# One kernel, a linear-attention block beside a gated feed-forward: K weights on ScalarE's DMA queue, normalisation shared out to VectorE and ScalarE, spare matmuls in another bank, a new order at the start, denominators spread differently

## The chip, the cores, the metric

One core of one Trainium2 chip runs the program. The metric is the device time of one execution in microseconds (us). Each comparison runs both kernels in alternation on the same chip. "Clock" is the mean share of TensorE's full clock that was granted in a run.

## The reference, cut to what matters

```python
xn = _layernorm(x)                        # x: 1 x 2048 x 576, bf16
def _A_ref(x, wqkv, wo):                  # linear attention, 32 heads of 18
    q, k, v = ...(x @ wqkv)...
    phi = lambda t: where(t > 0, t + 1, exp(t)) + 1e-6
    kv = einsum("bhsd,bhse->bhde", phi(k), v);  z = sum_s phi(k)
    o = (phi(q) @ kv) / (phi(q) . z + 1e-6)
    return o @ wo
def _B_ref(x, w_gate, w_up, w_down):      # F = 4608
    return (gelu(x @ w_gate) * (x @ w_up)) @ w_down
return x + _A_ref(xn, wqkv, wo) + _B_ref(xn, w_gate, w_up, w_down)
```

## The kernel before

The 2048 tokens are 16 tiles of 128. The kernel has an attention stage (to about 70 us), then four passes of 512 tokens, each with 18 blocks of gate and up matmuls and then the down projection. I call the steps of tile n: **Tn** its transposes on TensorE, **Kn** and **Qn** its ten K and ten Q matmuls with five in each half, **Gn** the seven matmuls that add its phi(k) and xn products up in PSUM. K0 needs x of tile 0: statistics on VectorE, reciprocal root on ScalarE, normalisation, T0, a copy out of PSUM in two parts (one on ScalarE, one on VectorE).

```python
nc.scalar.preload_act_table_set("natural_log_exp_and_others")
load_x(0, 1)            # SyncE's queue, in this order
load_x(1, 1)
load_w(1)               # K weights: rows 0-511, then rows 512-575
load_x(2, 2)
load_w(0)               # Q weights
load_x(4, 4)
...
def spin(count):        # spare matmuls, to keep TensorE's clock up
    nc.tensor.matmul(ps_all[:, 3, 0:P], lhsT=ident[:], rhs=ident[:], ...)
spin(NWARM)             # 38
...
def ln_norm(n, c0=0, c1=D):
    (nc.vector if n < TD else nc.gpsimd).tensor_scalar(...)   # TD = 3
...
TP_BANK = (3, 1, 0)     # PSUM banks of T0, T1, T2; G writes banks 0 to 3
```

The order of the attention stage on each engine is not written down; a list scheduler computes it in Python when the kernel is built. Each step has an engine, a duration, a rank and predecessors, and the loads are constants: the times from which x and the weights are believed to be there.

```python
X_AT = [2.95, 3.40, 6.20, 6.20] + [9.60] * 4
W_AT = {1: 5.60, 0: 7.90}
...
step(("stats", n, h), "DVE", 0.41, n - 2.2, after_x, ..., ready=x_at)
step(("aggr", n), "DVE", 0.21, n - 2.1, [("stats", n, 0), ("stats", n, 1)], ...)
...                     # cut: rstd, norm, tp, xnT, mm, exp, phi
step(("G", n), "PE", 0.75, n + 1.15, [("phi", n, 1, 0), ("phi", n, 1, 1)], ...)
```

Each engine then works through its instructions strictly in that order.

The denominators of the attention are computed on VectorE between the gated products of the feed-forward:

```python
nc.vector.tensor_tensor(out=hT[:, GUB * k + i, :], ...)    # gated product
if den_jobs and blk > 0:
    job, n = den_jobs.pop(0); job(n)
```

Of the kernel before, what the change touches and what calls it, by code (L numbers as in the profile page):

```python
# [8 lines left out]
ACT = mybir.ActivationFunctionType  # L9
ALU = mybir.AluOpType  # L10
BF16 = mybir.dt.bfloat16
F32 = mybir.dt.float32
# [3 lines left out]
P = 128  # L16
HP = 64
S = 2048
D = 576
# [3 lines left out]
NS = S // P  # L23
NF = F // P
# [11 lines left out]
GUB = 2  # L36
# [3 lines left out]
TD = 3  # L40
# [17 lines left out]
def kernel(  # L58
# [11 lines left out]
    nc = tc.nc  # L70
# [9 lines left out]
    persist = ctx.enter_context(tc.tile_pool(name="persist", bufs=1))  # L80
# [4 lines left out]
    ps_all = psum.tile([P, 8, 512], F32, name="ps_all")  # L85
# [4 lines left out]
    x_sb = persist.tile([P, NS, D], BF16, name="x_sb")  # L90

    def load_x(n0, cnt):
        nc.sync.dma_start(x_sb[:, n0:n0 + cnt, :], x_view[:, n0:n0 + cnt, :])  # L93
# [8 lines left out]
    wqkv_sb = apool.tile([P, KT, 3 * D], BF16, name="wqkv_sb")  # L102


    def load_w(which):
        c = slice(which * D, (which + 1) * D)
        nc.sync.dma_start(wqkv_sb[:, 0:4, c], A_wqkv[0:512, c].rearrange("(kt p) c -> p kt c", p=P))
        nc.sync.dma_start(wqkv_sb[0:HP, 4, c], A_wqkv[512:576, c])

    nc.scalar.preload_act_table_set("natural_log_exp_and_others")  # L110
    load_x(0, 1)
    load_x(1, 1)
    load_w(1)
    load_x(2, 2)
    load_w(0)
    load_x(4, 4)

    nc.vector.memset(wqkv_sb[HP:P, 4, :], 0.0)

    ident = const.tile([P, P], BF16, name="ident")  # L120
# [8 lines left out]
    def spin(count):  # L129

        for _ in range(count):
            nc.tensor.matmul(ps_all[:, 3, 0:P], lhsT=ident[:], rhs=ident[:], start=True, stop=True)

    spin(NWARM)

    xnT = persist.tile([P, KT, S], BF16, name="xnT")
# [15 lines left out]
    def load_gu(i, part):  # L152
# [17 lines left out]
    xn = apool.tile([P, NS, XW], BF16, name="xn")  # L170
# [9 lines left out]
        out=bm3, in_=bm3, compare_op=ALU.is_ge, fill=0.0,  # L180
# [3 lines left out]
        out=bm3, in_=bm3, compare_op=ALU.is_ge, fill=0.0,  # L184
# [8 lines left out]

    mv = persist.tile([P, NS, nc.vector.BN_AGGR_DIM], F32, name="mv")
    rstd = persist.tile([P, NS], F32, name="rstd")

    ln_raw = {}

    def ln_half(n, h):
        if h == 0:  # L200
            ln_raw[n] = asmall.tile([P, 2, nc.vector.BN_STATS_DIM], F32, name="stats")
        nc.vector.bn_stats(out=ln_raw[n][:, h, :], in_=x_sb[:, n, h * HALF:(h + 1) * HALF])  # L202

    def ln_aggr(n):
        nc.vector.bn_aggr(out=mv[:, n, :], in_=ln_raw[n][:])

    def ln_rstd(n):
        r = rstd[:, n:n + 1]
        nc.scalar.activation(out=r, in_=mv[:, n, 1:2], func=ACT.Ln, bias=eps_ln[:], scale=1.0)
        nc.scalar.activation(out=r, in_=r, func=ACT.Exp, scale=-0.5)  # L210

    def ln_norm(n, c0=0, c1=D):
        (nc.vector if n < TD else nc.gpsimd).tensor_scalar(  # L213
            out=xn[:, n, c0:c1], in0=x_sb[:, n, c0:c1], scalar1=mv[:, n, 0:1], scalar2=rstd[:, n:n + 1],
            op0=ALU.subtract, op1=ALU.mult,
        )
# [3 lines left out]
    def tp_bank(b):  # L220
        return ps_all[:, b, :].bitcast(BF16).rearrange("p (k t) -> p k t", t=P)
# [3 lines left out]
    def transposes(n, k0=0, k1=KT, b=None):  # L225
        b = TP_BANK[n] if b is None else b
        for kt in range(k0, k1):
            nc.tensor.transpose(tp_bank(b)[:, kt, :], xn[:, n, kt * P:(kt + 1) * P], ident[:])

    def tp_copy(n, k0=0, k1=KT, b=None, copy=acopy):  # L230
        b = TP_BANK[n] if b is None else b
        copy(out=xnT[:, k0:k1, n * P:(n + 1) * P], in_=tp_bank(b)[:, k0:k1, :])  # L232

    def dma_transposes(n):
        nc.sync.dma_start_transpose(xnT[:, :, n * P:(n + 1) * P], xn[:, n, 0:640])
# [162 lines left out]
    def step(name, *args, **kw):  # L398
        steps[name] = _Step(*args, **kw)

    X_AT = [2.95, 3.40, 6.20, 6.20] + [9.60] * 4
    W_AT = {1: 5.60, 0: 7.90}

    for n0 in (8, 12):
        step(("x", n0), "SP", 0.50, n0 - 5.5, [], lambda n0=n0: load_x(n0, 4), ready=8.5, tail=3.0)
    for n in range(NS):
        after_x = [("x", n // 4 * 4)] if n >= 8 else []
        x_at = X_AT[n] if n < 8 else 0.0
        for h in range(2):
            step(("stats", n, h), "DVE", 0.41, n - 2.2, after_x, lambda n=n, h=h: ln_half(n, h), ready=x_at)  # L410
        step(("aggr", n), "DVE", 0.21, n - 2.1, [("stats", n, 0), ("stats", n, 1)], lambda n=n: ln_aggr(n))
        step(("rstd", n), "ACT", 0.49, n - 2.1, [("aggr", n)], lambda n=n: ln_rstd(n))
        if n == 0:
            for i, (k0, k1, b, eng) in enumerate([(0, 3, 3, "ACT"), (3, KT, 2, "DVE")]):
                step(("norm", n, i), "DVE", 0.25, n - 2.1 + i / 10, [("rstd", n)],
                     lambda k0=k0, k1=k1: ln_norm(0, k0 * P, min(k1 * P, D)))
                step(("tp", n, i), "PE", 0.20, n - 1.5, [("norm", n, i)], lambda k0=k0, k1=k1, b=b: transposes(0, k0, k1, b))
                step(("xnT", n, i), eng, 0.45, n - 2.1, [("tp", n, i)],
                     lambda k0=k0, k1=k1, b=b, eng=eng: tp_copy(0, k0, k1, b, acopy if eng == "ACT" else vcopy))
            ready = [("xnT", n, 0), ("xnT", n, 1)]  # L420
        elif n < TD:
            step(("norm", n), "DVE", 0.42, n - 2.1, [("rstd", n)], lambda n=n: ln_norm(n))
            step(("tp", n), "PE", 0.30, n - 1.5, [("norm", n)], lambda n=n: transposes(n))
            step(("xnT", n), "ACT", 0.69, n - 1.5, [("tp", n)], lambda n=n: tp_copy(n))
            ready = [("xnT", n)]
        else:
            step(("norm", n), "POOL", 0.80, n - 2.1, [("rstd", n)], lambda n=n: ln_norm(n))
            step(("xnT", n), "SP", 2.30, n - 1.9, [("norm", n)], lambda n=n: dma_transposes(n), tail=0.4)
            ready = [("xnT", n)]
        for which, rank in ((1, n), (0, n + 0.6)):  # L430
            for h in range(2):
                r = rank + h / 100
                free = [("phi", n - 1, which, h)] if n else []
                step(("mm", n, which, h), "PE", 0.615, r, ready + free, lambda n=n, w=which, h=h: kq_mm(n, w, h),
                     ready=W_AT[which], tail=0.15)
                step(("exp", n, which, h), "ACT", 0.45, r + 0.10, [("mm", n, which, h)],
                     lambda n=n, w=which, h=h: kq_exp(n, w, h))
                step(("phi", n, which, h), "DVE", 0.43, r + 0.15, [("exp", n, which, h)],
                     lambda n=n, w=which, h=h: kq_phi(n, w, h))
        step(("G", n), "PE", 0.75, n + 1.15, [("phi", n, 1, 0), ("phi", n, 1, 1)], lambda n=n: g_accumulate(n, G_A))  # L440
    for i, (at, count) in enumerate([(5.75, 3), (6.15, 4)]):
        step(("spin", i), "PE", 0.1 * count, -1.0, [], lambda count=count: spin(count), ready=at)

    def in_order(steps):
# [89 lines left out]
    den_jobs = [(job, n) for n in range(NS) for job in (den_mul, den_inv, den_scale, den_transpose)]  # L534

    def gu_pair(sc, k):
        cs = slice(sc * SC, (sc + 1) * SC)
        blk = sc * (NF // GUB) + k
        wg, wu, wr = gu_blocks.pop(blk)
        units = []  # L540
        for i in range(GUB):
            b = [banks.next(), banks.next()]
            fcol = slice(i * P, (i + 1) * P)

            def lhs(a, rows, kt, fcol=fcol):
                if kt == 4:
                    return wr[rows, fcol]
                return (wg, wu)[a][rows, kt, fcol]

            u = _Unit([ps_all[:, b[0], :], ps_all[:, b[1], :]], lhs, lambda a, rows, kt: xnT[rows, kt, cs],  # L550
                      nc.sync if blk == 0 else nc.gpsimd)
            if blk > 0:
                load_gu(blk + NWBUF - 1, i)
            u.p1()
            units.append((b, u))
        if sc == 0 and k == 1:
            load_wo()
        elif sc == 0 and k >= 2:
            load_wd_slice()
        for i, (b, u) in enumerate(units):  # L560
            u.p2()
            gl = fwork.tile([P, SC], F32, name="gl")
            nc.scalar.activation(out=gl[:], in_=ps_all[:, b[0], :], func=ACT.Gelu_apprx_tanh)  # L563
            nc.vector.tensor_tensor(out=hT[:, GUB * k + i, :], in0=ps_all[:, b[1], :], in1=gl[:], op=ALU.mult)  # L564
            if den_jobs and blk > 0:
                job, n = den_jobs.pop(0)
                job(n)

# [76 lines left out]
```

## Time and profile before

| | before |
|---|---|
| median of 3 runs | 520.57 us (520.33 to 520.65) |
| span of the profiled execution | 517.8 us |
| TensorE busy | 510.4 us |
| T0, K0, Q0, G0 begin at | 5.5, 7.1, 9.4, 12.6 us |
| G0 to first gate/up matmul | 58.1 us |
| first gate/up matmul to first small product (m stage) | 70.3 us |
| first small product to first matmul of pass 2 | 42.6 us |
| pass 2 to the last matmul | 330.6 us |

The last rows cut TensorE's timeline at four marks. As TensorE sets the end nearly everywhere, a part of the change shows up as a difference of one of these distances. A line of a timeline reads: start us, duration us, engine, source line, operation, output<-input, shape, count, and in brackets the idle time before and what ended it. The lines of TensorE and of the waits are in the prediction. What the argument will need besides is VectorE's timeline of the kernel before:

```profile
3.00 1.19 DVE L202 BATCH_NORM_STATS2 stats<-x_sb 128x6 f32<-128x288 bf16 x3 [1.04 <-DMA x_sb<-in_A_x_dram]
4.11 0.19 DVE L205 BATCH_NORM_AGGREGATE mv<-stats 128x2 f32<-128x12 f32 x1
...
4.90 1.16 DVE L213 TENSOR_SCALAR xn<-x_sb,mv,rstd 128x384 bf16<-128x384 bf16 x3
```

The aggregate's start, 4.11, is what matters; further statistics between it and the normalisation are left out. Three statistics run ahead of tile 0's aggregate: two of tile 0 and the first of tile 1. Tile 1's x has landed by 3.75 (issued at 1.25, 2.5 us to landing), so this costs 0.37 us (one statistics instruction, from its start to the next one's) and no more.

### The profile page before, as it was taken

Reading aid. Unit: us, or ns where it says so; the run is one execution under the profiler, and the core shown is the slowest. Engines: PE = TensorE matmul, PEld = TensorE weight load, DVE = VectorE, ACT = ScalarE, POOL = GpSimd, SP = SyncE. Lnnn points to the kernel's source line nnn. Section 1 sums busy time; section 2 is a strip of 40 time slices with the busy share of each in tenths; the row PEclk is TensorE's granted clock in tenths of the full one; section 3 lists DMA queues with packets and bytes.
Section 4 is the critical chain, followed back from the end, with each engine's and each line's share of the span. In section 5 each row is a group of like instructions: output and inputs, shape, how many; then the busy total and the mean of one; then the engine's idle time right before and its main releaser. Section 6 shows DMA issues by size and latency. Waiting matters only on the chain.

```text
span 517.8 us, 10582 instructions
## 1 busy us (share of the span) xinstructions
PE 510.4 (99%) x4497; PEld 314.2 (61%) x4497; DVE 202.0 (39%) x407; ACT 133.5 (26%) x260; POOL 36.0 (7%) x32
## 2 busy tenths in 40 slices
PE   7999999999999999999999999999999999999997
PEld 6788864447577744444577644444777544445775
DVE  6895446666610146766301043343101233333100
ACT  5676523223320013323200032332000133232000
POOL 3995000000000000000000000000000000000000
PEclk9999999999999999999999999999999999999999
DMA  8237619999910046658500155555000455540000
GB/s 285 53 70 153 150 28 226 282 263 273 250 38 13 13 115 169 191 149 178 140 11 13 50 159 161 155 143 160 26 22 13 122 156 148 156 121 2 13 11 24
DMA packets 117785, 60.86 MB, mean 118 GB/s; under 512 B 24810, under 2 KB 117162, under 8 KB 117738
## 3 DMA queue, kind: packets, MB, share of 16 engines
q1 hardware_dynamic: 117738, 60.19, 45.0%
q8 instruction: 35, 0.57, 0.5%
q14 instruction: 12, 0.10, 0.1%
HBM read 52.79 MB, written 2.36 MB: 107 GB/s over the span
## 4 chain that ended last, share of the span: by engine, by line
PE 94%; DMA 3%; SPq 1%; ACT 1%; DVE 0%; POOL 0%; issue 0%
PE ps_all L298 53%; PE ps_all L592 27%; PE ps_all L243 6%; PE ps_all L597 4%; PE ps_all L274 4%; DMA wqkv_sb<-in_A_wqkv_dram 1%; DMA wr<-in_B_w_up_dram 1%; DMA xnT<-xn 1%; POOL xn L213 0%; SPq L93 0%; PE ps_all L345 0%; DVE hT L564 0%; PE ps_all L574 0%; ACT phi_e L250 0%; DVE den_t L358 0%
## 5 line engine op out<-in xcount | busy, mean ns | idle before, releaser
L298 PE MATMUL ps_all<-xnT,wg 64*128 64x512 bf16 x1152 | 272.4, 376 | 0.0
L298 PE MATMUL ps_all<-xnT,wu 64*128 64x512 bf16 x1152 | 270.8, 376 | 0.0
L563 ACT ACTIVATE gl<-ps_all 128x512 f32<-128x512 f32 x144 | 86.0, 597 | 314.1 <-PE ps_all L298 311.7
L564 DVE TENSOR_TENSOR hT<-ps_all,gl 128x512 bf16<-128x512 f32 x144 | 99.4, 690 | 145.7 <-ACT gl L563 145.4
L298 PEld LDWEIGHTS <-wu 64*128 64x128 bf16 x1152 | 108.1, 94 | 66.0
L298 PEld LDWEIGHTS <-wg 64*128 64x128 bf16 x1152 | 108.2, 94 | 65.6
L592 PE MATMUL ps_all<-wd_sb,hT 128*128 128x288 bf16 x1152 | 147.0, 286 | 0.0
L592 PEld LDWEIGHTS <-hT 128*128 128x128 bf16 x1152 | 112.3, 98 | 30.4 <-issue 2.0
L600 DVE TENSOR_TENSOR res<-ps_all,x_sb 128x288 bf16<-128x288 f32 x32 | 14.6, 458 | 143.6 <-PE ps_all L597 143.6
L298 PE MATMUL ps_all<-xnT,wr 64*128 64x512 bf16 x288 | 56.2, 376 | 0.1
L243 PE MATMUL ps_all<-wqkv_sb,xnT 128*128 128x288 bf16 x320 | 42.5, 286 | 1.3 <-DMA wqkv_sb<-in_A_wqkv_dram 0.9
L243 PEld LDWEIGHTS <-xnT 128*128 128x128 bf16 x320 | 30.4, 98 | 9.0 <-issue 1.1
L250 ACT ACTIVATE phi_e<-ps_all,neg 128x288 f32<-128x288 f32 x64 | 31.6, 499 | 15.1 <-PE ps_all L243 11.4
L213 POOL TENSOR_SCALAR xn<-x_sb,mv,rstd 128x576 bf16<-128x576 bf16 x13 | 29.6, 2287 | 8.7 <-ACT rstd L210 8.7
L298 PEld LDWEIGHTS <-wr 64*128 64x128 bf16 x288 | 14.9, 94 | 17.6 <-DMA wr<-in_B_w_up_dram 0.8
L597 PE MATMUL ps_all<-m_sb,pqT 126*128 126x288 bf16 (+1 forms) x160 | 24.9, 286 | 0.0
L274 PE MATMUL ps_all<-hT,xn 128*128 128x288 bf16 (+4 forms) x176 | 22.6, 275 | 0.3 <-ACT xnT L232 0.3
L274 PEld LDWEIGHTS <-xn 128*128 128x128 bf16 (+1 forms) x176 | 17.6, 101 | 4.4 <-issue 0.5
L255 DVE SCALAR_TENSOR_TENSOR pq<-phi_e,ps_all 128x288 bf16<-128x288 f32 x32 | 14.5, 452 | 10.1 <-ACT phi_e L250 9.8
L597 PEld LDWEIGHTS <-pqT 126*128 126x128 bf16 (+1 forms) x160 | 15.5, 97 | 4.1
L255 DVE SCALAR_TENSOR_TENSOR hT<-phi_e,ps_all 128x288 bf16<-128x288 f32 x32 | 14.4, 453 | 3.4 <-ACT phi_e L250 3.0
L202 DVE BATCH_NORM_STATS2 stats<-x_sb 128x6 f32<-128x288 bf16 x32 | 13.0, 441 | 2.1 <-DMA x_sb<-in_A_x_dram 2.1
(51 smaller groups left out, 100.5 us busy)
## 6 DMA issues: line engine op xcount, KB each, us to landing
wg<-in_B_w_gate_dram SPq DMA_DIRECT2D x72, 256.0 KB, 3.1
wu<-in_B_w_up_dram SPq DMA_DIRECT2D x72, 256.0 KB, 3.7
wd_sb<-in_B_w_down_dram SPq DMA_DIRECT2D x12, 432.0 KB, 6.0
wr<-in_B_w_gate_dram SPq DMA_DIRECT2D x72, 32.0 KB, 2.9
wr<-in_B_w_up_dram SPq DMA_DIRECT2D x72, 32.0 KB, 3.2
out_dram<-res SPq DMA_DIRECT2D x15, 144.0 KB, 1.8
wqkv_sb<-in_A_wqkv_dram SPq DMA_DIRECT2D x3, 576.0 KB, 5.3
x_sb<-in_A_x_dram SPq DMA_DIRECT2D x3, 576.0 KB, 8.2
```

The source lines that it names most:

```text
L202: nc.vector.bn_stats(out=ln_raw[n][:, h, :], in_=x_sb[:, n, h * HALF:(h + 1) * HALF])
L213: (nc.vector if n < TD else nc.gpsimd).tensor_scalar(out=xn[:, n, c0:c1], in0=x_sb[:, n, c0:c1], scalar1=mv[:, n, 0:1], scalar2=rstd[:, n: ...
L243: nc.tensor.matmul(ps_all[:, KQ_BANK[which] + hf, :HALF], lhsT=xnT[:, kt, n * P:(n + 1) * P], rhs=wqkv_sb[:, kt, c:c + HALF], start=(kt == ...
L250: nc.scalar.activation(out=e[:], in_=ps_all[:, KQ_BANK[which] + hf, :HALF], func=ACT.Exp, bias=neg1[:], scale=1.0,)
L255: nc.vector.scalar_tensor_tensor(out=(pq, pk)[which][:, n, hf * HALF:(hf + 1) * HALF], in0=e_tiles[n, which, hf][:], scalar=1.0, in1=ps_al ...
L274: nc.tensor.matmul(ps_all[:m, b, col:col + w], lhsT=xn[:, n, j0:j0 + m], rhs=pk[:, n, d0:d0 + w], start=(n == 0 and col == 0), stop=(n == ...
L298: return nc.tensor.matmul(self.outs[i], lhsT=self.lhs(i, rows, kt), rhs=self.rhs(i, rows, kt), start=start, stop=stop, skip_group_check=True,)
L563: nc.scalar.activation(out=gl[:], in_=ps_all[:, b[0], :], func=ACT.Gelu_apprx_tanh)
L564: nc.vector.tensor_tensor(out=hT[:, GUB * k + i, :], in0=ps_all[:, b[1], :], in1=gl[:], op=ALU.mult)
L592: nc.tensor.matmul(acc, lhsT=hT[:, f, j * P:(j + 1) * P], rhs=wd_sb[:, f, hs], start=(f == 0), stop=False,)
L597: nc.tensor.matmul(acc, lhsT=pqT[:rows, c, ts_], rhs=m_sb[:rows, c, hs], start=False, stop=(c == NCH - 1),)
L600: nc.vector.tensor_tensor(out=res[:, hs], in0=acc, in1=x_sb[:, n, hs], op=ALU.add)
```

## The change

The intent: K weights arrive sooner from a second queue; SyncE issues the rest sooner; spare matmuls no longer wait for a bank that ScalarE reads; K0 goes ahead of T1; GpSimd's 2.3 us normalisation goes to faster engines; the denominators keep clear of the end of a pass.

```diff
-    def load_w(which):
+    def load_w(which, on=nc.sync):
...
+    load_x(0, 1)
+    load_w(1, nc.scalar)
     nc.scalar.preload_act_table_set("natural_log_exp_and_others")
-    load_x(0, 1)
     load_x(1, 1)
-    load_w(1)
     load_x(2, 2)
...
-            nc.tensor.matmul(ps_all[:, 3, 0:P], lhsT=ident[:], ...
+            nc.tensor.matmul(ps_all[:, 7, 0:P], lhsT=ident[:], ...
...
+    def ln_bias(n):       # GpSimd: nbias = -mean * rstd, 128x1
+    def ln_norm_act(n):   # ScalarE: Identity, bias=nbias, scale=rstd
...
-        (nc.vector if n < TD else nc.gpsimd).tensor_scalar(
+        nc.vector.tensor_scalar(
...
-    X_AT = [2.95, 3.40, 6.20, 6.20] + [9.60] * 4
-    W_AT = {1: 5.60, 0: 7.90}
+    X_AT = [3.30, 3.80, 5.60, 5.60] + [9.00] * 4
+    W_AT = {1: 5.00, 0: 7.60}
...
-            step(("tp", n), "PE", 0.30, n - 1.5, ...
+            step(("tp", n), "PE", 0.30, n - 0.9, ...
...
-            step(("norm", n), "POOL", 0.80, n - 2.1, [("rstd", n)], ...
+            if n % 2:
+                step(("bias", n), "POOL", 0.15, n - 2.1, [("rstd", n)], ...
+                step(("norm", n), "ACT", 0.65, n - 2.1, [("bias", n)], ...
+            else:
+                step(("norm", n), "DVE", 0.43, n - 2.1, [("rstd", n)], ...
...                        # cut: durations of exp, phi, xnT; 3+3 spares instead of 3+4
-            if den_jobs and blk > 0:
+            if den_jobs and 0 < k < NF // GUB - 1:
```

More of the change, by code (lines that the diff above doesn't have):

```diff
@@ L102 @@
     wqkv_sb = apool.tile([P, KT, 3 * D], BF16, name="wqkv_sb")
-    def load_w(which):
+    def load_w(which, on=nc.sync):
         c = slice(which * D, (which + 1) * D)
-        nc.sync.dma_start(wqkv_sb[:, 0:4, c], A_wqkv[0:512, c].rearrange("(kt p) c -> p kt c", p=P))
-        nc.sync.dma_start(wqkv_sb[0:HP, 4, c], A_wqkv[512:576, c])
+        on.dma_start(wqkv_sb[:, 0:4, c], A_wqkv[0:512, c].rearrange("(kt p) c -> p kt c", p=P))
+        on.dma_start(wqkv_sb[0:HP, 4, c], A_wqkv[512:576, c])
+    load_x(0, 1)
+    load_w(1, nc.scalar)
     nc.scalar.preload_act_table_set("natural_log_exp_and_others")
-    load_x(0, 1)
     load_x(1, 1)
-    load_w(1)
     load_x(2, 2)
@@ L131, in spin @@
         for _ in range(count):
-            nc.tensor.matmul(ps_all[:, 3, 0:P], lhsT=ident[:], rhs=ident[:], start=True, stop=True)
+            nc.tensor.matmul(ps_all[:, 7, 0:P], lhsT=ident[:], rhs=ident[:], start=True, stop=True)
     spin(NWARM)
@@ L195 @@
     rstd = persist.tile([P, NS], F32, name="rstd")
+    nbias = persist.tile([P, NS], F32, name="nbias")
     ln_raw = {}
@@ L210, in ln_rstd @@
         nc.scalar.activation(out=r, in_=r, func=ACT.Exp, scale=-0.5)
+    def ln_bias(n):
+        nc.gpsimd.tensor_scalar(
+            out=nbias[:, n:n + 1], in0=mv[:, n, 0:1], scalar1=rstd[:, n:n + 1], scalar2=-1.0, op0=ALU.mult, op1=ALU.mult,
+        )
+    def ln_norm_act(n):
+        nc.scalar.activation(
+            out=xn[:, n, 0:D], in_=x_sb[:, n, :], func=ACT.Identity, bias=nbias[:, n:n + 1], scale=rstd[:, n:n + 1],
+        )
     def ln_norm(n, c0=0, c1=D):
-        (nc.vector if n < TD else nc.gpsimd).tensor_scalar(
+        nc.vector.tensor_scalar(
             out=xn[:, n, c0:c1], in0=x_sb[:, n, c0:c1], scalar1=mv[:, n, 0:1], scalar2=rstd[:, n:n + 1],
@@ L422 @@
             step(("norm", n), "DVE", 0.42, n - 2.1, [("rstd", n)], lambda n=n: ln_norm(n))
-            step(("tp", n), "PE", 0.30, n - 1.5, [("norm", n)], lambda n=n: transposes(n))
+            step(("tp", n), "PE", 0.30, n - 0.9, [("norm", n)], lambda n=n: transposes(n))
             step(("xnT", n), "ACT", 0.69, n - 1.5, [("tp", n)], lambda n=n: tp_copy(n))
@@ L426 @@
         else:
-            step(("norm", n), "POOL", 0.80, n - 2.1, [("rstd", n)], lambda n=n: ln_norm(n))
-            step(("xnT", n), "SP", 2.30, n - 1.9, [("norm", n)], lambda n=n: dma_transposes(n), tail=0.4)
+            if n % 2:
+                step(("bias", n), "POOL", 0.15, n - 2.1, [("rstd", n)], lambda n=n: ln_bias(n))
+                step(("norm", n), "ACT", 0.65, n - 2.1, [("bias", n)], lambda n=n: ln_norm_act(n))
+            else:
+                step(("norm", n), "DVE", 0.43, n - 2.1, [("rstd", n)], lambda n=n: ln_norm(n))
+            step(("xnT", n), "SP", 2.10, n - 1.9, [("norm", n)], lambda n=n: dma_transposes(n), tail=0.6)
             ready = [("xnT", n)]
@@ L435 @@
                      ready=W_AT[which], tail=0.15)
-                step(("exp", n, which, h), "ACT", 0.45, r + 0.10, [("mm", n, which, h)],
+                step(("exp", n, which, h), "ACT", 0.49, r + 0.10, [("mm", n, which, h)],
                      lambda n=n, w=which, h=h: kq_exp(n, w, h))
-                step(("phi", n, which, h), "DVE", 0.43, r + 0.15, [("exp", n, which, h)],
+                step(("phi", n, which, h), "DVE", 0.44, r + 0.15, [("exp", n, which, h)],
                      lambda n=n, w=which, h=h: kq_phi(n, w, h))
         step(("G", n), "PE", 0.75, n + 1.15, [("phi", n, 1, 0), ("phi", n, 1, 1)], lambda n=n: g_accumulate(n, G_A))
-    for i, (at, count) in enumerate([(5.75, 3), (6.15, 4)]):
+    for i, (at, count) in enumerate([(5.80, 3), (6.20, 3)]):
         step(("spin", i), "PE", 0.1 * count, -1.0, [], lambda count=count: spin(count), ready=at)
```

## The prediction

> **What bounds the kernel now.** I read the page's busy times first, then all waits of TensorE over the whole span, then the chain of waits, and last the timeline of each engine from 0 to 20 us, because the diff edits only the attention stage's beginning and one condition in the feed-forward loop. Busy times and groups:
>
> ```profile
> span 517.8 us, 10582 instructions
> PE 510.4 (99%) x4497; PEld 314.2 (61%) x4497; DVE 202.0 (39%) x407; ACT 133.5 (26%) x260; POOL 36.0 (7%) x32
> L213 POOL TENSOR_SCALAR xn<-x_sb,mv,rstd 128x576 bf16<-128x576 bf16 x13 | 29.6, 2287 | 8.7 <-ACT rstd L210 8.7
> ```
>
> TensorE is busy 510.4 of 517.8 us. The change takes away none of its real matmuls, so all it can win lies in the other 7.4 us, plus the spare matmuls that stand on the path. GpSimd's 29.6 us of normalising looks expensive but lies beside TensorE's work. Waits of TensorE (us in total, times, longest):
>
> ```profile
> PE ps_all L132 <- POOL ident masks.py:199: 1.4, 1, 1.4
> PE ps_all L243 <- DMA wqkv_sb<-in_A_wqkv_dram: 0.9, 1, 0.9
> PE ps_all L574 <- DVE hT L564: 0.6, 1, 0.6
> PE ps_all L132 <- ACT xnT L232: 0.4, 1, 0.4
> PE ps_all L243 <- DMA xnT<-xn: 0.3, 1, 0.3
> PE ps_all L274 <- ACT xnT L232: 0.3, 1, 0.3
> ```
>
> They sum to 3.9 us. The first (the identity matrix, 1.42 us) is untouched; the tail after the last matmul (514.5 to 517.8) too. So 2.5 us of waits are in reach. TensorE's timeline puts them in place (start, duration):
>
> ```profile
> 6.45 0.55 PE L132 MATMUL ps_all<-ident 128*128 128x128 bf16 x7 [0.39 <-ACT xnT L232]
> 6.83 0.44 PE L228 MATMUL ps_all<-ident,xn 128*128 128x128 bf16 x5
> 7.11 1.39 PE L243 MATMUL ps_all<-wqkv_sb,xnT 128*128 128x288 bf16 x10
> 9.41 2.00 PE L243 MATMUL ps_all<-wqkv_sb,xnT 128*128 128x288 bf16 x15 [0.91 <-DMA wqkv_sb<-in_A_wqkv_dram]
> 12.58 0.90 PE L274 MATMUL ps_all<-hT,xn 128*128 128x288 bf16 x7 [0.28 <-ACT xnT L232]
> 18.21 1.40 PE L243 MATMUL ps_all<-wqkv_sb,xnT 128*128 128x288 bf16 x10 [0.30 <-DMA xnT<-xn]
> ```
>
> Read it as a sequence: spare matmuls, transposes of token tile 1 (T1), K of tile 0 (K0) at 7.11, then 0.91 us until the Q weights land, Q0 at 9.41. Whatever is won ahead of 9.41 without earlier Q weights is lost in that wait. The chain agrees; its first piece that counts is that load:
>
> ```profile
> 3.41 5.96 DMA wqkv_sb<-in_A_wqkv_dram
> 9.41 2.01 PE ps_all L243 x15
> ```
>
> After 18.6 TensorE has no gap until 126 us (busy 10.00 of every 10 us), so what is won before then reaches the end unchanged.
>
> **What the Trainium skill says.** (1) "DMA: Bandwidth & Descriptors", section "Issuing engines are not separate DMA queues": queues of several issuers interleave on the same 16 DMA engines, and a second issuer saves only sequencer time. The trace agrees that this time matters here: SyncE's issues follow each other at about 0.5 us (0.80, 1.25, 1.72, 2.19, 2.79, 3.41), and the DMAs moved 118 and 194 GB/s in 3.0 to 3.5 and 3.5 to 4.0 us against 378 and 403 in 4.5 to 5.5: early on there is too little queued. (2) "ScalarE: Activation LUTs", section "What ACT_TABLE_LOAD costs": an instruction with immediate scale and bias takes 186 ns + 0.833 ns per element; each per-partition operand adds about 93 ns; a table load about 1283 ns. The trace has 1.28 us for the load, 0.20 and 0.30 us for the two 128x1 activations, 499 ns for the exponential (the page's formula gives 280+240=520). Section "Table sets: the hidden batching unit": cheap functions such as identity are in every set, so I expect no further load; no run yet shows it. (3) "GPSIMD Engine Reference", section 3.1, has GpSimd slower than VectorE elementwise; here 2287 against 424 ns for the same 128x576 normalisation. (4) "PSUM — Partial Sum Buffer", section "PSUM bank collisions raise a hardware error": guard by bank. The 0.39 us wait is that guard: the spares write bank 3, which ScalarE is reading.
>
> **The change, part by part.**
>
> (a) K weights on ScalarE's queue. Two issues (0.43+0.56 us) leave SyncE, so tile 2's x goes out at about 1.72 instead of 2.79, Q at about 2.4 instead of 3.41. K itself starts at about 0.8, not 1.72. The table load ends near 3.1 instead of 2.07; its first user runs at 4.33, so that is hidden. All bytes up to Q still share 16 engines: 0.15+0.15+0.66+0.29+0.66=1.91 MB. What can be won is the thin stretch from 2 to 4 us, where 0.42 MB moved; at 350 GB/s it would be 0.7 MB, so at most 0.28 MB, worth 0.8 us. I take 0.5 us: Q at about 8.9 instead of 9.37. The price: x of tiles 0 and 1 share with K. The author's constants move them by 0.35 and 0.40 us, tile 2 and K by -0.6, Q by -0.3; as shifts I find these plausible.
>
> (b) Spares in bank 7: the 0.39 us wait goes. There are 6 instead of 7.
>
> (c) T1 behind K0: K0 no longer waits for T1 (0.28 us start to start). But the new constants also change VectorE's order. Following the list scheduler by hand, tile 2's first statistics (believed in at 5.60) now go ahead of VectorE's half copy of tile 0's transpose; before, that copy (6.09) ran first and the statistics waited until 7.47. So K0 would hang on tile 2's x. I expect it at about 6.7; plus 0.37 (statistics, start to start), 0.29 (copy) and 0.1, K0 at about 7.45, later than now; K0 and T1 take 1.25+0.35, so Q0 at about 9.05. Gain there: 0.36 us, not the 0.9 that the label suggests.
>
> (d) The 0.28 us wait: G0 writes bank 0, out of which ScalarE copies T2. By hand the order stays K1 first half, T2, K1 second half, G0, but the copy now has fewer exponentials ahead of it. G0 at about 12.0 instead of 12.58: 0.55 us gained so far in all.
>
> (e) Normalising: 13 GpSimd operations become 6 on VectorE (0.42 us) and 7 on ScalarE. With two per-partition operands I estimate 186+2x93+0.833x576=852 ns from the ScalarE page (the code assumes 650), and a 128x1 bias on GpSimd, 0.2 us. Tile 3 is ready at least 1 us sooner, so the 0.30 us wait at 18.21 goes. Engine load between 20 and 40 us: VectorE 17.9 of 20, ScalarE 15.1 of 20. Per tile (3.2 us) the addition averages 0.2 and 0.4 us. That fits because both run ahead: VectorE falls to 5.5 of 10 after 40 us. Gain: 0.30 us.
>
> (f) The denominators: no job in the last block of each pass, none in the first of the second pass. In the chain before, 0.66 us of den_t stands between the last two gated products, and the second (142.23) holds up TensorE:
>
> ```profile
> 140.87 0.69 DVE hT L564
> 141.57 0.66 DVE den_t L358
> 142.23 0.61 DVE hT L564
> 142.88 0.28 PE ps_all L574
> ```
>
> Without it the second product starts when its gelu ends (141.11+0.60), so at about 141.75 to 141.8; 0.41 us gained of the 0.56 us wait. Jobs elsewhere are hidden: each later pass's 648 matmuls take 70.04 us.
>
> Sum: 0.55 + 0.30 + 0.41 = 1.26 us, 0.24%: 520.57 - 1.26 = 519.3; I put 519.4, leaving 0.1 for small new waits.
>
> **Rivals.** First, x of tile 2 takes the place of the Q weights as the wait. For it: the order worked out in (c), and two rings sharing the engines. Against: its issue is a microsecond earlier. If it lands at 7.4, Q0 starts near 9.7, the start loses 0.3, and the total is 520.1 to 520.5. Second, ScalarE or VectorE becomes the bound in 12 to 40 us: K needs the previous tile's result out of the same bank, and a 0.85 us operation stands in an in-order queue. Slack is about 3.2-0.6-1.3=1.3 us. For it: VectorE's 90%. Against: its operations overlap at the ends (0.45 us long, 0.37 apart). A wait of 0.1 us per tile would cost 1.3 us and leave 520.5 to 521. Third, bandwidth rather than issue limits Q: then (a) gives nothing, only (e) and (f) remain, 519.9. Fourth, everything fits: Q at 8.7, no gap up to 18 us, all 0.56 us of (f): 518.5. The 0.4 us stall at about 133 us on the up-projection's last rows (part of TensorE's busy time) may also shift by itself either way.
>
> **Range and chances.** The three runs before spread 0.3 us. Rival four bounds it below, rivals one and two above: 518.5 to 520.5. A gain over 2% would need 10.4 us, more than all idle time; a loss over 2% would need a fresh wait in each tile of 0.7 us. So within 2% is nearly certain.
>
> **What would show it.** Right: VectorE's first statistics of tile 2 ahead of its xnT copy, and K0 between 7.2 and 7.8; Q0 between 8.8 and 9.4; no wait of spare matmuls on ScalarE; the waits on the xnT transposes gone; the wait of L574's counterpart at most 0.2 us; one table load at the start; ScalarE's normalisation near 0.8 us; TensorE still 10.00 of 10 us from 20 to 60. Wrong: any TensorE wait on phi or exponentials inside 12 to 60 us, K0 beyond 8 us, or Q weights still landing at 9.4.

## The result, and the profile after

The changed kernel took 519.02 us (median of 4 runs, 518.40 to 519.97) against 520.49 us. A ratio is the mean time of a kernel's fast runs over that of the kernel before in the same rounds, so not quite the ratio of these medians: 0.9973, with a 95% interval of 0.9956 to 0.9991. In a second job it was 0.9989 (0.9973 to 1.0006). The mean of its ten runs is 519.6 us. The total lies in the predicted range; how it came about is another matter.

The changed kernel's page, and three groups by line:

```profile
span 516.6 us, 10582 instructions
...
PE 509.7 (99%) x4496; PEld 309.7 (60%) x4496; DVE 202.6 (39%) x413; ACT 137.3 (27%) x267; POOL 8.3 (2%) x26
...
L219 ACT ACTIVATE xn<-x_sb,nbias,rstd 128x576 bf16<-128x576 bf16 x7 | 6.0, 859 | 0.5 <-POOL nbias L214 0.4
...
L214 POOL TENSOR_SCALAR nbias<-mv,rstd 128x1 f32<-128x1 f32 x7 | 1.9, 264 | 37.5 <-ACT rstd L211 27.1 <-DVE pq L266 10.4
```

GpSimd's 29.6 us of normalising have become 1.9 us; ScalarE pays 0.86 us for a tile. TensorE's waits (us in total, times, longest) are now these four, all of them:

```profile
PE ps_all L239 <- DVE xn L224: 1.8, 1, 1.8
PE ps_all L132 <- POOL ident masks.py:199: 1.4, 1, 1.4
PE ps_all L285 <- ACT xnT L243: 0.2, 1, 0.2
PE ps_all L589 <- DVE hT L579: 0.2, 1, 0.2
```

The waits on the Q weights, of the spare matmuls on a bank and on the transposed tile from the DMA are gone. Those of G0 on the copy by ScalarE and of the small products on the last gated product have shrunk, from 0.28 to 0.17 us and from 0.6 to 0.2. In place of the others stands a new one of 1.8 us. TensorE's timeline shows where:

```profile
7.44 0.53 PE L239 MATMUL ps_all<-ident,xn 128*128 128x128 bf16 x5 [1.78 <-DVE xn L224]
...
8.35 1.40 PE L254 MATMUL ps_all<-wqkv_sb,xnT 128*128 128x288 bf16 x10
...
9.87 2.00 PE L254 MATMUL ps_all<-wqkv_sb,xnT 128*128 128x288 bf16 x15
...
12.93 0.90 PE L285 MATMUL ps_all<-hT,xn 128*128 128x288 bf16 x7 [0.17 <-ACT xnT L243]
```

T0 starts at 7.44 instead of 5.54 and K0 at 8.35 instead of 7.11. VectorE's timeline says why:

```profile
3.57 0.82 DVE L203 BATCH_NORM_STATS2 stats<-x_sb 128x6 f32<-128x288 bf16 x2 [1.61 <-DMA x_sb<-in_A_x_dram]
5.83 0.46 DVE L203 BATCH_NORM_STATS2 stats<-x_sb 128x6 f32<-128x288 bf16 x1 [1.44 <-DMA x_sb<-in_A_x_dram]
6.21 0.19 DVE L206 BATCH_NORM_AGGREGATE mv<-stats 128x2 f32<-128x12 f32 x1
...
7.00 0.62 DVE L224 TENSOR_SCALAR xn<-x_sb,mv,rstd 128x384 bf16<-128x384 bf16 x2
```

The order is that of before: two statistics of tile 0, one of tile 1, then tile 0's aggregate. But tile 1's x was issued at 1.25 us, behind no more than tile 0's x on its own queue, and landed only at 5.81, 4.56 us after its issue instead of 2.5: it shared the engines with 0.66 MB of K weights from the other queue. VectorE stood 1.44 us in front of it with tile 0's finished statistics in hand.

By the four marks, the profiled difference of 1.2 us splits as follows.

| | before | after | difference |
|---|---|---|---|
| start to G0 | 12.6 | 12.9 | +0.3 |
| G0 to first gate/up matmul | 58.1 | 57.5 | -0.6 |
| to first small product | 70.3 | 69.8 | -0.5 |
| to first matmul of pass 2 | 42.6 | 42.2 | -0.4 |
| to the end | 334.2 | 334.2 | 0 |

So the start, of which the prediction expected the largest gain, shows none. Its +0.3 us is no exact figure, though: a second profile of the kernel before (e9) has G0 at 13.1, which would make it -0.2; neither is the gain of 0.55 us that was forecast. And the changed kernel's ten runs (four here, six in e1) scatter by 2.9 us. The experiments ask three things: what holds the start; where the scatter comes from; what each part is worth.

### The profile page after: what moved, and what is told of

It reads as the page before. It is cut to its first block, busy times and chain, and to the rows that moved or that the text cites. A ratio compares the mean times of both kernels' runs of the same rounds, so it can differ in the third digit from the quotient of the medians.

```text
span 516.6 us, 10582 instructions
## 1 busy us (share of the span) xinstructions
PE 509.7 (99%) x4496; PEld 309.7 (60%) x4496; DVE 202.6 (39%) x413; ACT 137.3 (27%) x267; POOL 8.3 (2%) x26
## 4 chain that ended last, share of the span: by engine, by line
PE 97%; DMA 1%; ACT 0%; DVE 0%; issue 0%; SPq 0%
PE ps_all L309 54%; PE ps_all L607 27%; PE ps_all L254 8%; PE ps_all L285 4%; PE ps_all L612 4%; DMA x_sb<-in_A_x_dram 1%; PE ps_all L356 0%; ACT xnT L243 0%; PE ps_all L589 0%; PE ps_all L239 0%; DVE hT L579 0%; ACT gl L578 0%; DVE stats L203 0%; DVE res L615 0%; SPq L93 0%
## 5 line engine op out<-in xcount | busy, mean ns | idle before, releaser
L309 PE MATMUL ps_all<-xnT,wr 64*128 64x512 bf16 x288 | 54.7, 376 | 0.0
L254 PE MATMUL ps_all<-wqkv_sb,xnT 128*128 128x288 bf16 x320 | 42.2, 286 | 0.1
L261 ACT ACTIVATE phi_e<-ps_all,neg 128x288 f32<-128x288 f32 x64 | 30.1, 497 | 9.6 <-PE ps_all L254 6.9
L388 DVE SCALAR_TENSOR_TENSOR pn<-pq,den_d 128x504 bf16<-128x504 bf16 (+1 forms) x32 | 13.1, 449 | 0.0
```

The source lines that it names most:

```text
L254: nc.tensor.matmul(ps_all[:, KQ_BANK[which] + hf, :HALF], lhsT=xnT[:, kt, n * P:(n + 1) * P], rhs=wqkv_sb[:, kt, c:c + HALF], start=(kt == ...
L261: nc.scalar.activation(out=e[:], in_=ps_all[:, KQ_BANK[which] + hf, :HALF], func=ACT.Exp, bias=neg1[:], scale=1.0,)
L309: return nc.tensor.matmul(self.outs[i], lhsT=self.lhs(i, rows, kt), rhs=self.rhs(i, rows, kt), start=start, stop=stop, skip_group_check=True,)
L388: nc.vector.scalar_tensor_tensor(out=pn[:].rearrange("p (c t) -> p c t", t=P)[:, c0:c1, :nh * DH].rearrange("p c (h e) -> p c h e", e=DH), ...
```

## The experiments

Twelve runs were made, two of them without an edit; all compared correct with the reference. (The second profile of the kernel before is a single run, whose state is unknown.) The stages of all profiles, in us:

| profile | T0 | K0 | G0 | G0 to gate/up | to small product | to pass 2 | span |
|---|---|---|---|---|---|---|---|
| before | 5.5 | 7.1 | 12.6 | 58.1 | 70.3 | 42.6 | 517.8 |
| e9, before again | 5.5 | 7.6 | 13.1 | 58.1 | 70.5 | 42.6 | 518.5 |
| after | 7.4 | 8.4 | 12.9 | 57.5 | 69.8 | 42.2 | 516.6 |
| e1, after again | 7.3 | 8.2 | 14.4 | 57.5 | 69.8 | 42.2 | 518.1 |
| e3 | 7.5 | 8.4 | 14.7 | 58.1 | 69.8 | 42.2 | 519.0 |
| e4 | 7.2 | 8.2 | 12.7 | 57.5 | 69.8 | 42.6 | 516.8 |
| e5 | 7.4 | 8.4 | 12.9 | 57.5 | 69.8 | 42.2 | 516.6 |
| e6 | 5.5 | 7.5 | 13.1 | 57.4 | 69.8 | 42.2 | 516.7 |
| e7 | 5.8 | 6.7 | 12.8 | 56.5 | 69.8 | 42.2 | 515.5 |
| e8 | 5.8 | 6.9 | 13.1 | 56.3 | 70.1 | 42.2 | 515.9 |
| e10 | 7.8 | 9.4 | 15.4 | 58.2 | 70.4 | 42.5 | 520.7 |
| e11 | 7.8 | 9.0 | 13.6 | 57.5 | 69.8 | 42.2 | 517.3 |
| e12 | 5.8 | 6.9 | 13.2 | 56.4 | 69.8 | 42.2 | 515.8 |

In e7, e8 and e12 G0 stands later in TensorE's order, so their two columns around G0 are to be added up before comparing.

### e1_again: the scatter

No edit.

> The changed kernel once more, unedited, for its spread: its four runs lie between 518.40 and 519.97 us, those of the kernel before within 0.32 us. Theory A (the new 1.78 us pause of TensorE ahead of its first transposes sometimes costs it its full clock for a while): runs fall into groups, most near 518.5, some 1 to 1.5 us above with a mean granted clock of 0.997 or so. Theory B (the spread is in transfers later on): clock 1.0 in all runs, and the slow profile shows waits on transfers. Ratio to the kernel before 0.997.

Six runs: 520.08, 520.11, 519.68, 519.95, 521.29, 518.60 us, with clocks 0.995, 0.995, 1.0, 0.997, 0.999, 1.0; ratio 0.9989. This time the profile caught a run of low clock. First the view of stretches of e1_again (after the span: length, busy time of TensorE, weight loads, VectorE, ScalarE, GpSimd; then granted clock, DMA share, GB/s), then one stretch of the first profile:

```profile
8.50:9.50 1.00, 1.00 (x6) 0.64 (x5) 0.85 (x4) 0.00 (x0) 0.00 (x0) 0.50 1.03 424
...
10.50:11.50 1.00, 1.00 (x9) 0.82 (x8) 1.00 (x5) 0.18 (x2) 0.00 (x0) 0.50 1.04 429
...
12.00:13.00 1.00, 1.00 (x11) 0.80 (x9) 0.49 (x2) 1.00 (x4) 0.00 (x0) 1.00 0.00 0
```

```profile
8.50:9.50 1.00, 1.00 (x10) 0.80 (x9) 0.97 (x4) 0.32 (x1) 0.00 (x0) 1.00 1.01 383
```

The matmuls of 8.5 to 9.5 us are 6 instead of 10: the clock is 0.50, from about 8.2 to 11.6 us, and K0 takes 2.58 us instead of 1.40. G0 begins at 14.4 instead of 12.9, everything after it runs as in the first profile. So one such drop costs 1.5 us. It begins 0.9 us after a pause of 2.02 us. Two more profiles below show such a drop, after pauses of 1.98 (e3) and 2.12 us (e10); the first profile and e4's had pauses of 1.78 and 1.59 us and no drop. Theory A holds for the runs of low clock. The runs of 519.68 and 521.29 us have no low clock on record, and no profile caught one of them: what slowed those is open, as it is for single runs of e3 (521.54), e4 (520.15) and e10 (523.45). The other half of the expectation failed: in this job the eleven runs of the kernel before lie between 519.70 and 521.72 us, not within 0.32, at clocks of 0.999 to 1.0. So medians of a few runs that differ by less than a microsecond decide little, and the marks carry most of what follows.

Why about half of the runs? The starts of the single matmuls in the traces give a hint. The first spare matmuls follow each other at 107 ns and later ones at 56 ns; the change came at 4.8 us in e1's profile and at 5.3 in e3's (there seen only in the last gap, 100 ns). The drops lie at 8.2 to 11.6 and at 8.7 to 12.1 us: each 3.4 us after the change, and 3.4 us long. In the 3.4 us ahead of the drop TensorE was busy for 1.38 us in both. A clock that is set anew every 3.4 us by how busy TensorE was would fit this, and so the same pause would count in some runs and not in others. That is argued from two profiles; no run tests it.

### e2_true_landing and e8_true_landing_valid: give the scheduler true landing times

```diff
-    X_AT = [3.30, 3.80, 5.60, 5.60] + [9.00] * 4
-    W_AT = {1: 5.00, 0: 7.60}
+    X_AT = [3.30, 6.00, 6.60, 6.60] + [9.00] * 4
+    W_AT = {1: 5.00, 0: 8.50}
```

> Only constants of the list scheduler are changed, to the landing times that the changed kernel's trace shows (x of tile 1 6.0 instead of 3.8, of tiles 2 and 3 6.6 instead of 5.6, Q 8.5 instead of 7.6), so VectorE's first statistics of tile 1 stand behind tile 0's normalisation and no longer ahead of its aggregate. Theory A (tile 1's x, landing at 5.8, holds tile 0 through VectorE's in-order queue): first transposes at 5.6 to 6.0 instead of 7.44, K0 at 6.5 to 7.0 instead of 8.35, Q0 at 8.5 to 8.9 instead of 9.9; about 1.0 us faster than the changed kernel (517.5 to 517.9) and a spread as small as that of the kernel before. Rival (the K weights or the order of matmuls hold the start anyway): K0 stays beyond 8 us and the time is within 0.3 us of the changed kernel's.

517.73 us (517.55 to 518.00, 5 runs), ratio 0.9947, clock 0.999 to 1.0. T0 began at 5.8 and K0 at 6.7; Q0 waited 0.35 us for its weights and began at 8.45. No transfer was edited; what changes at the start is that tile 1's statistics no longer stand ahead of tile 0's aggregate. But the kernel is not valid. The orders show it: the scheduler does not know that T2 and G0 share bank 0. In e2 G0 runs at 9.95 us and T2, which by the kernel's text writes over what G0 has summed in that bank, at 12.14. (In the changed kernel T2 runs at 11.71, ahead of G0 at 12.93.) The comparison with the reference passed all the same. So the order was made legal and run again:

```diff
-        step(("G", n), "PE", 0.75, n + 1.15, [("phi", n, 1, 0), ("phi", n, 1, 1)], ...
+        step(("G", n), "PE", 0.75, n + 1.15, [("phi", n, 1, 0), ("phi", n, 1, 1)]
+             + ([("xnT", 1), ("xnT", 2)] if n == 0 else []), ...
```

> The kernel of e2_true_landing again, in which G0 was found to run ahead of tile 2's transposes and to lose its sums in the bank that they share, although the comparison passed; here the scheduler knows of that. Theory A: start as in e2 (transposes 5.8, K0 6.7, Q weights at 8.45), G0 later than there, time 517.6 to 518.2. Rival (e2's gain came from the illegal order): 518.5 or more.

517.66 us (517.44 to 518.29, 5 runs), ratio 0.9949, clock 0.999 to 1.0. The gain was not the illegal order's. Tile 0's aggregate and transposes in e8's profile:

```profile
4.57 0.21 DVE L206 BATCH_NORM_AGGREGATE mv<-stats 128x2 f32<-128x12 f32 x1
...
5.81 0.71 PE L239 MATMUL ps_all<-ident,xn 128*128 128x128 bf16 x5 [0.15 <-DVE xn L224]
```

That tile 1's x holds the start through VectorE's queue is shown: with the order alone changed, the aggregate goes from 6.21 to 4.57 and T0 from 7.4 to 5.8. Four landing times were put right at once, so this experiment by itself doesn't say that it was tile 1's; e7, which brings tile 1's x sooner, and e10, which brings it later, do.

### e3_norm_on_gpsimd: undo the normalisation

```diff
-        nc.vector.tensor_scalar(
+        (nc.vector if n < TD else nc.gpsimd).tensor_scalar(
...                     # and the steps of tiles 3 to 15 as before
```

> The changed kernel with the normalisation of tiles 3 to 15 back on GpSimd, as before. Theory A (moving it was worth 0.7 us, since two transposed tiles came late before, 0.30 us as a shown wait of the matmuls and the rest inside TensorE's busy time): 0.6 to 0.8 us slower than the changed kernel, G of tiles 1 and 3 more than 6.4 us apart again. Rival (as predicted, only the shown wait of 0.30 us was at stake): 0.3 us slower. Second rival: no difference, since tiles are late by the start anyway (K0 at 8.35) and GpSimd has caught up.

520.95 us (519.98 to 521.54, 6 runs), ratio 1.0007. Four of the six runs have a clock of 0.997, so the times don't compare cleanly with e1's; the marks do. G0 to the first gate/up matmul takes 58.1 us again instead of 57.5, so the part is worth 0.6 us. TensorE's timeline of e3:

```profile
17.88 0.91 PE L285 MATMUL ps_all<-hT,xn 128*128 128x288 bf16 x7
...
20.30 1.40 PE L254 MATMUL ps_all<-wqkv_sb,xnT 128*128 128x288 bf16 x10 [0.28 <-DMA xnT<-xn]
21.53 0.91 PE L285 MATMUL ps_all<-hT,xn 128*128 128x288 bf16 x7
...
24.98 0.91 PE L285 MATMUL ps_all<-hT,xn 128*128 128x288 bf16 x7
```

From G to G are 3.65 and 3.45 us where the undisturbed distance is 3.20; only 0.28 us of that is shown as a matmul's wait. The weight loads show the rest: in the kernel before, as in e3, they waited twice for a transposed tile, 1.0 us in all.

```profile
PEld L243 <- DMA xnT<-xn: 1.0, 2, 0.6
```

### e4_den_old: undo the denominators' condition

```diff
-            if den_jobs and 0 < k < NF // GUB - 1:
+            if den_jobs and blk > 0:
```

> The changed kernel with the old condition for the denominators' jobs. Theory A: the wait of the small products on the last gated product of the first pass is back at 0.5 to 0.6 us instead of 0.2, and the kernel is 0.4 us slower. Rival: no difference in time, because the down-projection catches up elsewhere.

520.19 us (518.50 to 520.53, 6 runs), ratio 0.9986; three of six runs at 0.996 or 0.997, so again the time decides nothing, the rival included. The wait on the last gated product is 0.6 us again, and the distance from first small product to pass 2 is 42.6 instead of 42.2. The part is worth 0.4 us.

### e5_pause_filled: is it the pause?

```diff
-NWARM = 38
+NWARM = 68
```

> The changed kernel with 68 instead of 38 spare matmuls at the start, so that TensorE is busy until shortly before its first transposes at about 7.4 us; nothing else moves. Theory A (the 1.6 to 2.0 us pause there is what lets TensorE's granted clock fall to half for some 3.4 us in about half of the runs): mean clock 0.999 or 1.0 in every run, none of the runs at 0.995 to 0.997, median near 518.6 to 519.0. Rival (the clock falls for another reason, such as the later small waits or the chip's power): the same share of runs at 0.995 to 0.997 and the median near 520.0.

518.62 us (518.29 to 519.19, 5 runs), ratio 0.9968, clock 0.999 to 1.0 in all. The start is as late as in the changed kernel, only TensorE is not idle in it:

```profile
1.43 5.67 PE L132 MATMUL ps_all<-ident 128*128 128x128 bf16 x68 [1.43 <-POOL ident masks.py:199]
7.44 0.52 PE L239 MATMUL ps_all<-ident,xn 128*128 128x128 bf16 x5 [0.35 <-DVE xn L224]
...
8.36 1.40 PE L254 MATMUL ps_all<-wqkv_sb,xnT 128*128 128x288 bf16 x10
```

Thirty useless matmuls win 1.1 us by the ratios against e1 (0.9968 against 0.9989) and 0.3 us against the first job (0.9973); the intervals overlap, so the clocks say more than the times. Over all twelve kernels and the first job: of the 26 runs of kernels with a pause of 1.6 to 2.1 us ahead of T0 (the changed kernel, e3, e4, e10), 14 have a clock of 0.993 to 0.997; of the 35 runs of the others (e2, e5 to e8, e11, e12) none is below 0.999, nor is any run of the kernel before. The edit alone has small counts: none of nine runs with the pause filled (e5, e11), four of ten without. Together the counts show that the pause is what lets the clock fall.

### e6_norm_den_only: two parts alone

The kernel before, with the normalisation part and the denominators' condition of the change, and nothing else of it.

> The kernel before with two parts of the change alone: normalisation on VectorE and ScalarE in turn, and the denominators' new condition. Loads, spare matmuls, ranks and constants of the start are those of before. Theory A: 0.6 us from the normalisation and 0.4 us from the denominators, 1.0 us faster than the kernel before, the clock at 0.999 to 1.0, first transposes at 5.5 and K0 at 7.1: faster than the whole change, whose start costs. Rival (the gain needs the earlier loads): less than 0.5 us.

518.41 us (517.64 to 518.51, 5 runs), ratio 0.9959, clock 0.999 to 1.0. That is 1.96 us less than the kernel before in the same rounds by the medians, more than the 1.0 us of theory A: the two parts show as 0.7 and 0.4 us at their marks, and the stretch up to the first small product has 69.8 us instead of 70.3 (see e9). What is left of the 1.96 us, some 0.4 us, is within the scatter of the kernel before. By the ratio these two parts alone do better than the whole change (0.9973 and 0.9989); against the first of these the intervals overlap (0.9946 to 0.9971 and 0.9956 to 0.9991).

### e10_k_queue_only: the first part alone

```diff
+    load_x(0, 1)
+    load_w(1, nc.scalar)
     nc.scalar.preload_act_table_set("natural_log_exp_and_others")
-    load_x(0, 1)
     load_x(1, 1)
-    load_w(1)
```

> The kernel before with the first part of the change alone: the K weights on ScalarE's queue ahead of its table load, tile 1's x behind them, all scheduling constants as before. Theory A (tile 1's x now lands at 5.8 and its first statistics stand ahead of tile 0's aggregate, here too): first transposes at 7.2 to 7.5 with a pause of 1.6 to 2.0 us ahead of them, Q weights at 8.5 with nobody waiting; 0.5 to 1.0 us slower than the kernel before at full clock, and some runs with mean clock 0.995 to 0.997, 1.5 us slower still. Rival (earlier Q weights are a gain by themselves): faster than the kernel before by 0.3 us or more.

523.01 us (522.56 to 523.63, 4 runs), ratio 1.0051, 95% interval 1.0037 to 1.0064; clocks 0.997, 1.0, 0.997, 0.993. TensorE and VectorE in its profile:

```profile
7.78 0.53 PE L228 MATMUL ps_all<-ident,xn 128*128 128x128 bf16 x5 [2.12 <-DVE xn L213]
```

```profile
6.18 0.46 DVE L202 BATCH_NORM_STATS2 stats<-x_sb 128x6 f32<-128x288 bf16 x1 [1.58 <-DMA x_sb<-in_A_x_dram]
```

The same picture with the old constants: tile 1's statistics wait for x, TensorE pauses for 2.12 us, the clock falls (0.50 from 9.7 to 13.1 us). The part taken for the change's main gain costs 2.7 us by itself. Up to G0 the profile explains that: 15.4 against 12.6 or 13.1. But 0.5 to 1.0 us had been expected at full clock, and the one run at 1.0 took 523.45 us, more than two of the runs at low clock; what it lost, no profile shows. The new constants do not cause the hold; that order was there before, harmless.

### e11_spares_bank3: what the free bank is worth

e5 with the spares back in bank 3, since e5's clock is steady.

```diff
-            nc.tensor.matmul(ps_all[:, 7, 0:P], lhsT=ident[:], ...
+            nc.tensor.matmul(ps_all[:, 3, 0:P], lhsT=ident[:], ...
```

> The kernel of e5_pause_filled, whose clock is steady, with the spare matmuls back in bank 3, out of which ScalarE copies tile 0's transposes. Theory A: the six spares wait for that copy and then stand 0.34 us ahead of K0, which moves from 8.36 to about 8.7 to 8.8, and 0.35 to 0.45 us are lost, since nothing behind K0 waits for anything else. Rival (the 0.4 us wait of before was hidden behind the Q weights and the bank does not matter): less than 0.15 us.

519.03 us (518.70 to 519.27, 4 runs), ratio 0.9973; e5 had 0.9968, which is within the noise. The profile of e11 has T0 itself 0.38 us later (its 68 spares took 6.55 us), so I compare from T0 on: K0 follows after 1.22 instead of 0.92 us and G0 after 5.79 instead of 5.49. The free bank is worth 0.30 us there, a little less than expected.

### e9_before_again: the stall at 133 us, and the start once more

No edit of the kernel before.

> The kernel before, unedited, for a second profile. Its first profile has a stall of 0.4 to 0.5 us near 133 us on the last rows of the up-projection's weights, which no profile of the changed kernel or of its variants has. If the stall belongs to the kernel's order of issues it is there again (first block of gate and up matmuls to the first of the small products 70.3 us); if it is chance of that execution's transfers, that stretch takes 69.8 us as in all others.

The stall is there again: 70.5 us to the first small product, the weight loads waiting 1.1 us in all for the up-projection's last rows. e10 has it (70.4), but neither e3 nor e4, e6 or after (69.8), and e8 a little of it (70.1). So chance alone is unlikely, but it goes with no single part: the old normalisation alone (e3) doesn't bring it, nor the old denominators alone (e4), while both with an early start (before) or a late one (e10) do. What decides it is open.

The start differs too: K0 at 7.56 us instead of 7.11 and G0 at 13.06 instead of 12.58, in the same kernel. In the first profile the spare matmuls pass from 107 to 56 ns apart at 5.1 us, in this one only at 7.2, and those ahead of K0 run slowly; the clock column reads 1.00 in both. (It is 7.0 us in e6, whose K0 came at 7.5 instead of the 7.1 expected.) So a mark at the start is good to about half a microsecond, unless one looks at this first.

### e7_x1_first and e12_k_rest_on_sync: the better version

```diff
     load_x(0, 1)
+    load_x(1, 1, nc.scalar)
     load_w(1, nc.scalar)
     nc.scalar.preload_act_table_set("natural_log_exp_and_others")
-    load_x(1, 1)
...
-    X_AT = [3.30, 3.80, 5.60, 5.60] + [9.00] * 4
-    W_AT = {1: 5.00, 0: 7.60}
+    X_AT = [3.40, 4.30, 6.20, 6.20] + [9.00] * 4
+    W_AT = {1: 5.90, 0: 8.30}
...                     # and G0 behind xnT 1 and 2, as in e8
```

> The changed kernel with tile 1's x on ScalarE's queue ahead of the K weights, the constants set to landing times expected from the traces, and G0 made to wait for the transposes of tiles 1 and 2 in the list scheduler (it shares banks with them). Theory A (the start is held by tile 1's x in VectorE's queue): first transposes at 5.6 to 5.9, K0 at 6.6 to 6.9, G0 at 11.6 to 12.0 instead of 12.9; 1.0 to 1.3 us faster than the changed kernel's fast runs, 517.3 to 517.7, and clock 0.999 to 1.0. Rival (K weights, now issued 0.45 us later, land after 7.5): K0 near 8 and no gain.

517.33 us (517.22 to 517.46, 5 runs), ratio 0.9941 (0.9928 to 0.9953), clock 0.999 to 1.0: faster than both kernels, with a spread of 0.24 us. (Against e8's 0.9949 it is within the noise. G0 was expected at 11.6 to 12.0 us and came at 12.85.) VectorE and TensorE in its profile:

```profile
3.74 0.82 DVE L203 BATCH_NORM_STATS2 stats<-x_sb 128x6 f32<-128x288 bf16 x2 [1.78 <-DMA x_sb<-in_A_x_dram]
4.59 0.21 DVE L206 BATCH_NORM_AGGREGATE mv<-stats 128x2 f32<-128x12 f32 x1
```

```profile
5.83 0.52 PE L239 MATMUL ps_all<-ident,xn 128*128 128x128 bf16 x5 [0.37 <-DVE xn L224]
...
7.87 0.91 PE L254 MATMUL ps_all<-wqkv_sb,xnT 128*128 128x288 bf16 x6 [0.46 <-DMA wqkv_sb<-in_A_wqkv_dram]
```

The aggregate follows its statistics at once. K0's first four matmuls start at 6.75; the fifth waits 0.46 us for the last 64 rows of the K weights. e12 sends those rows over SyncE's queue instead:

```diff
-        on.dma_start(wqkv_sb[0:HP, 4, c], A_wqkv[512:576, c])
+        nc.sync.dma_start(wqkv_sb[0:HP, 4, c], A_wqkv[512:576, c])
```

> The kernel of e7_x1_first with the last 64 rows of the K weights on SyncE's queue right behind tile 0's x, since K0's fifth matmul waited 0.46 us for them in e7. Theory: they land before 7.2, K0 runs through from 6.75, and up to 0.4 us are gained, 516.9 to 517.3. Rival (a later wait, Q weights or tile 1's transpose, takes it): within 0.1 us of e7's 517.3.

517.47 us (517.37 to 517.73, 6 runs), ratio 0.9944. K0 runs through from 6.87, and then Q0 waits 0.55 us for its weights and starts at 9.20: the rival was right within the noise, a wait in the K weights was turned into one for the Q weights.

## Why the prediction was right or wrong, point by point

The total was predicted at 519.4 us and came out at 519.0 (519.6 over both jobs). That is a right sum of partly wrong terms, and so in part luck.

**What bounds the kernel.** Right. TensorE's real matmuls are untouched, its waits are what moved, and between 20 and 60 us it stayed at 10.00 of every 10 us in spite of a fuller VectorE and ScalarE. That rival fell.

**(a), earlier loads.** The mechanism, more bytes in flight early, was right, and a little stronger than estimated: the first 512 rows of the Q weights landed at 8.5 us (issued at 2.19, 6.3 us to landing) and the last 64 at 8.8 (2.67 and 6.1), where 8.9 was expected. Tile 2's x landed at 6.6 (predicted 6.7). The price was the step that failed. The prediction took the 0.40 us for tile 1's x as "plausible"; it is 2.06 us (5.81 against 3.75). Here the two queues did not share the engines by need: a small transfer that everything waits for got its bytes beside a large one that nobody needed yet.

**(c), the order.** The prediction looked for an x that stands in VectorE's way, found tile 2's ahead of a copy (they do run there, at 7.54 ahead of 8.00 us, but that x had landed long before), and overlooked tile 1's ahead of tile 0's aggregate, earlier in the same order and visible in the profile of before, where it is the third of the three statistics. So K0 came at 8.35 instead of 7.45, Q0 at 9.87 instead of 9.05. "K0 beyond 8 us" was the prediction's own sign of being wrong, and it was. Its first rival named the right kind of wait with the wrong tile.

**(b) and (d).** The spares' wait is gone; with K0 bound by tile 0, the free bank is worth 0.30 us (e11). G0 came at 12.93 instead of 12.0. At full clock the start lost 0.3 us, or won 0.2 against e9, where 0.55 was to be gained.

**What no step had.** The pause of 1.8 us ahead of T0, which the failed step makes, lets TensorE's clock fall to half in 14 of the 26 runs of the kernels that have it, at 1.5 us each (e1). The prediction looked at the length of idle time and not at what idle time does to the clock.

**(e), normalisation.** Right in kind, mis-sized: 0.6 us instead of 0.30 (e3). The prediction read matmul waits only; half the loss showed as weight loads waiting for a transposed tile, while TensorE still counted as busy. (Its "no gap until 126 us" is not quite so either: the kernel before has 9.92 busy us of 10 between 20 and 30.) The cost of ScalarE's instruction was estimated well: 852 ns against 859. No further table load appeared: each kernel has two, the second near 60 us.

**(f), denominators.** Right: 0.41 us predicted, 0.4 measured, the residual wait 0.2 us as forecast.

**The stall at 133 us.** It was named as able to shift "by itself either way" and given nothing in the sum. It gave 0.5 us, and its cause is not settled (e9).

So in the profile +0.3 for the start, -0.6, -0.5 and -0.4, which makes 1.2: close to the 1.26 us predicted, by the luck of errors that cancel.

## What to carry to other kernels

Before a transfer moves to a second queue, list what the first queue still carries that the critical path needs, and where its consumers stand in the in-order queues: here one statistics instruction that waited for 144 KB of x undid the gain. When an order is computed from assumed landing times, put the landing times of the trace back into it, and tell it of shared banks; that alone, without moving a byte, took a further 1.2 to 2.1 us off the changed kernel (e8's 0.9949 against 0.9973 and 0.9989); against e5, whose clock is steady, it is 1.0 us (0.9968). And count a pause of TensorE not only by its length: fill it, or expect some runs at half clock after it.

## What the Trainium skill lacked or had wrong

- "TensorE: Matmul & The Clock Gate", the section "Why this matters for your kernels", advises against idle gaps of more than about 3 us between bursts of matmuls, and Part 1 has the clock fall after an idle window of about 3.4 us. Here kernels with pauses of 1.6 to 2.1 us have the fall in 14 of 26 runs; three profiles show it, after pauses of 1.98, 2.02 and 2.12 us. The 3.4 us ahead of the fall were no idle window: in e1 and e3 they held 1.38 us of matmuls. The half clock itself and its length agree: 0.50, for 3.4 us.
- "DMA: Bandwidth & Descriptors", section "Issuing engines are not separate DMA queues", says that a second issuer saves only issue time. It gives no figure for what sharing does to a small transfer on the first queue: 144 KB took 4.56 us to land beside 0.66 MB of the second queue, 2.5 us without.
- "GPSIMD Engine Reference", section 3.1, gives a ratio to VectorE of 1.96 for an fp32 tensor_tensor. For this bf16 tensor_scalar of 128x576 it is 5.4 (2287 against 424 ns), and a 128x1 one takes 264 ns, which the section doesn't have. (Times of GpSimd in these profiles are rough.)
